# Softmax of a sparse attention: maxima subtracted by VectorE into SBUF, one exponential per kind of head and pair, row sums by VectorE

## The chip, the core and the metric

The kernel runs on one core of a Trainium2 chip. A core has TensorE (matmuls, PE in the profile), VectorE (DVE), ScalarE (ACT), GpSimd (POOL) and SyncE (SP), which issues the DMAs. Matmuls write into PSUM, here eight banks of 128 x 512 float32; SBUF is the working memory. The metric is the device time of one execution in microseconds; a kernel's time is the median of its runs.

## The reference

It is an attention with sparse masks, followed by two expert layers on its output. `q`, `k` and `v` have the shape 4 x 8 x 576 x 64; the layers have 2304 tokens of width 512 and 2048 hidden features.

```python
scores = scale * np.matmul(q, k.transpose(0, 1, 3, 2))
rel = pos[:, None] - pos[None, :]
mask_local = (rel >= 0) & (rel < 32)
mask_strided = (rel >= 0) & (pos[None, :] % 32 == pos[:, None] % 32)
# heads 0 to 3 take mask_local, heads 4 to 7 mask_strided
scores = np.where(masks[None], scores, -1e9)
scores = scores - np.max(scores, axis=-1, keepdims=True)
attn = np.exp(scores)
attn = attn / (np.sum(attn, axis=-1, keepdims=True) + 1e-09)
x = heads_side_by_side(np.matmul(attn, v))
h = x @ moe_w_in;  x = (h * sigmoid(1.702 * h)) @ moe_w_out
h = x @ moe2_w_in; return (h * sigmoid(h)) @ moe2_w_out
```

## The kernel before

The work is cut into eight chunks, one for each batch and half of the sequence. In each chunk `attention(c, b)` computes the attention and `chunk(c)` the first layer for its 288 tokens; the second layer follows for all tokens, from about 500 us on. Chunk 0 runs in float32. From chunk 1 on each operand is split into a high and a low float16 half, and a product takes three matmuls.

A chunk's attention has four pairs: pair `i` joins local head `i` (g = 0) and strided head `i` (g = 1). A local head has three blocks of 96 queries by 128 keys. A strided head has four blocks of 72 x 72 in a first half (s = 0) and five of 63 x 126 in a second half (s = 1); of these five, four lie in one PSUM bank and one in another. There are 32 pairs in all, 16 for each half.

A pair passes these steps. TensorE writes mask and scores into PSUM banks (`scores`, L643 and L662). VectorE takes the negated row maxima (`maxes`, L671). The maxima are multiplied by the score scale (`scaled`, L681 on ScalarE or L683 on VectorE). ScalarE then runs one exponential for each block, seven or eight a pair (`exps`, L690): it reads the bank, adds the scaled maximum as a bias, writes to `sml` (local) or `sms` (strided) in SBUF, and collects the row sum through its accumulator into `sus`. VectorE adds 1e-9 to the sums and divides by a power of two, PSC (L696), and takes the reciprocal (L699). GpSimd multiplies the probabilities by it (L708). TensorE transposes them (L715), ScalarE or VectorE brings them from the bank to `ptt` (L722 to L730), VectorE makes the low half (L732), and TensorE multiplies with v (`times_v`, L757 for chunk 0, L764 else). The results go to `x` (L784 to L797).

In `chunk`, sixteen hidden tiles of the first layer take twelve matmuls each (L846; L843 in chunk 0), with the activation on ScalarE (L854) and the split on ScalarE (L383) and VectorE (L390). The second product has sixteen groups of twelve (L877; L873 in chunk 0). Beside this run the conversions of the first layer's weights (ScalarE L429 and L281, VectorE L286 and L288, GpSimd L293, norms on TensorE L301), their splits (L390), the parking of the second layer's weights in HBM and the sums that its fast products need ("factors", L505 and L528).

The order of all this is made ahead by a `Planner`, a list scheduler: every step is a task with a cost in microseconds for each engine that may run it, a priority (a due time), the tasks that it follows, and the buffers that it takes and uses. Eight PSUM banks are one pool (`ps`), the score tiles are the pools `sl` and `st` of four slots each. Where two engines are given, the one that comes free first takes the task. So a change of costs or of dependences moves other tasks too. Each engine works through its list in order. In this first part the planner's order is final for all five engines; the second layer has a planner of its own.

## Time and profile before

| | |
|---|---|
| median of 3 runs | 891.87 us (891.73 to 893.89) |
| span of the profiled execution, first to last instruction | 885.8 us |
| TensorE busy | 852.4 us, 96% |
| VectorE busy | 669.3 us, 76% |
| ScalarE busy | 591.8 us, 67% |
| GpSimd busy | 415.7 us, 47% |
| TensorE busy from 30 to 66, 66 to 91 and 433 to 500 us | 36.00, 23.39 and 66.87 us |

The profiled execution's own time outside its span is not given; the median of the runs is 6.1 us above the span. Busy time counts stretches in which at least one instruction of the engine is under way. Matmuls overlap one another, so a busy TensorE is not yet one at its full rate, and the rate of its groups is read beside it. A wait names the engine and line whose semaphore came last. The chain follows the work that ended last back to its cause, step by step.

### The profile page before, as it was taken

The numbers are of one execution on the slowest core, as the hardware profiler recorded it, in microseconds if no ns is written. First come the engines' busy times: TensorE is split into PE (matmuls) and PEld (weight loads), VectorE is DVE, ScalarE is ACT, GpSimd is POOL, SyncE is SP. The second block draws the span as 40 slices with busy tenths as digits, with TensorE's granted clock in tenths as the row PEclk, the third lists the DMA queues.
The fourth block names the chain that finished last, engine by engine and source line by source line (L and its number), as shares of the span: only waits on it lengthen the run. The fifth ranks groups of instructions, "written<-read, shape, count | busy, mean of one in ns | idle before, by whom it ended". The sixth has DMA issues, their size and how long they took to land.

```text
span 885.8 us, 21399 instructions
## 1 busy us (share of the span) xinstructions
PE 852.4 (96%) x8198; PEld 720.9 (81%) x8198; DVE 669.3 (76%) x1198; ACT 591.8 (67%) x1410; POOL 415.7 (47%) x430
## 2 busy tenths in 40 slices
PE   5999897899999899999999999999999999999997
PEld 4976675787888787788888888888888998888886
DVE  3798888988659778999475372788888699968742
ACT  5788688999959979899469342464555487646420
POOL 4666664553322345965222162577887563212110
PEclk9999999999999999999999999999999999999999
DMA  9857443455337277384210283467676989756501
GB/s 316 255 176 207 132 127 100 127 174 187 97 103 211 84 242 236 119 250 163 71 50 9 77 322 108 165 225 232 200 231 205 309 274 304 255 179 211 195 36 48
DMA packets 86086, 155.27 MB, mean 175 GB/s; under 512 B 8416, under 2 KB 45792, under 8 KB 84960
## 3 DMA queue, kind: packets, MB, share of 16 engines
q1 hardware_dynamic: 85984, 153.91, 53.6%
q8 instruction: 64, 1.05, 0.5%
q14 instruction: 38, 0.31, 0.1%
HBM read 100.40 MB, written 53.48 MB: 174 GB/s over the span
## 4 chain that ended last, share of the span: by engine, by line
PE 72%; DVE 11%; ACT 8%; DMA 4%; issue 2%; POOL 1%; SPq 0%; DVEq 0%; ACTq 0%; POOLq 0%
PE aps L1157 9%; PE aps L1268 8%; PE aps L877 6%; PE aps L846 5%; PE gps L877 5%; PE hps L1157 5%; PE gps L1157 4%; PE hps L1268 4%; PE gps L1268 4%; PE hps L846 3%; PE gps L846 2%; DMA rk<-in_k_dram 2%; PE hps L877 2%; ACT sms L690 1%; ACT sml L690 1%
## 5 line engine op out<-in xcount | busy, mean ns | idle before, releaser
L1157 PEld LDWEIGHTS <-wf 128*128 128x128 f16 x1680 | 150.6, 98 | 15.3
L1268 PEld LDWEIGHTS <-wf 128*128 128x128 f16 x1512 | 147.6, 98 | 18.6 <-issue 1.1
L846 PEld LDWEIGHTS <-regA 128*128 128x128 f16 x1152 | 113.1, 99 | 37.0 <-issue 5.3
L877 PEld LDWEIGHTS <-regB 128*128 128x128 f16 x1152 | 108.7, 98 | 27.4 <-issue 0.5
L973 POOL TENSOR_TENSOR tt<-tt 128x256 f32<-128x256 f32 (+2 forms) x84 | 74.7, 900 | 47.2 <-DVE wf L980 17.7
L846 PE MATMUL aps<-x,regA 128*128 128x288 f16 x600 | 80.0, 287 | 1.8 <-DVE g L390 1.4
L877 PE MATMUL aps<-g,regB 128*128 128x288 f16 x576 | 77.7, 286 | 0.5 <-ACT sml L690 0.5
L968 ACT ACTIVATE wf<-tt,xsg 128x512 f16<-128x512 f32 x87 | 58.1, 713 | 26.5 <-PE hps L1268 7.0
L293 POOL TENSOR_TENSOR wm<-wm 128x512 int32<-128x512 int32 x32 | 42.8, 1336 | 64.0 <-DVE wm L288 45.8
L980 DVE SCALAR_TENSOR_TENSOR wf<-tt,xsg,wf 128x512 f16<-128x512 f32 x87 | 71.5, 870 | 0.0
L708 POOL TENSOR_TENSOR sml<-sml,sus 96x384 f32<-96x384 f32 x32 | 30.4, 950 | 82.2 <-DVE sus L699 69.5
L877 PE MATMUL gps<-g,regB 128*128 128x288 f16 x432 | 58.9, 286 | 0.0
L1268 PE MATMUL aps<-regA,wf 128*128 128x256 f16 x456 | 53.2, 273 | 0.1
L1157 PE MATMUL aps<-xfa,wf 128*128 128x256 f16 (+1 forms) x528 | 53.1, 256 | 0.0
L1169 ACT ACTIVATE tt<-tt 128x512 f32<-128x512 f32 x39 | 24.4, 625 | 29.4 <-DVE tt L1164 29.3
L846 PE MATMUL gps<-x,regA 128*128 128x288 f16 x288 | 40.4, 291 | 3.3 <-DVE g L390 1.7
L968 ACT ACTIVATE wf<-regB,xsg 128x512 f16<-128x512 f32 x39 | 27.0, 715 | 19.6 <-DMA regB<-g_scratch 8.3
L1157 PE MATMUL aps<-g,wf 128*128 128x256 f16 x324 | 38.8, 273 | 0.0
L846 PE MATMUL hps<-x,regA 128*128 128x288 f16 x264 | 35.6, 286 | 1.6 <-DVE wm L288 1.6
L1268 PE MATMUL aps<-regB,wf 128*128 128x256 f16 x312 | 37.0, 273 | 0.0
L708 POOL TENSOR_TENSOR sms<-sms,sus 72x288 f32<-72x288 f32 (+1 forms) x32 | 34.5, 1079 | 0.0
L1268 PE MATMUL hps<-regA,wf 128*128 128x256 f16 x264 | 32.4, 273 | 0.8 <-DVE x L1283 0.5
(365 smaller groups left out, 2155.3 us busy)
## 6 DMA issues: line engine op xcount, KB each, us to landing
tt<-g_scratch SPq DMA_DIRECT2D x76, 256.0 KB, 4.1
g_scratch<-tt SPq DMA_DIRECT2D x64, 256.0 KB, 2.8
w<-in_moe_w_out_dram SPq DMA_DIRECT2D x24, 512.0 KB, 4.4
rv<-in_v_dram SPq DMA_DIRECT2D x8, 1024.0 KB, 5.2
regB<-in_moe_w_in_dram SPq DMA_DIRECT2D x16, 512.0 KB, 8.4
w<-in_moe_w_in_dram SPq DMA_DIRECT2D x16, 512.0 KB, 3.7
w_scratch<-wm SPq DMA_DIRECT2D x32, 256.0 KB, 3.1
regB<-g_scratch SPq DMA_DIRECT2D x32, 256.0 KB, 4.1
```

Source lines behind the costliest of these rows:

```text
L293: nc.gpsimd.tensor_tensor(out=di, in0=m.bitcast(I32), in1=di, op=ALU.add)
L690: nc.scalar.activation(out=sm[0:nq, e * nk:e * nk + nk], in_=bank[0:nq, (e % 4) * nk:(e % 4) * nk + nk], func=AF.Exp, bias=nms[0:nq, sl.id ...
L708: nc.gpsimd.tensor_tensor(out=smv(), in0=smv(), in1=sus[0:nq, sl.idx, 3 * g:3 * g + nb, None].to_broadcast([nq, nb, nk]), op=ALU.mult), [k ...
L846: nc.tensor.matmul(o, lhsT=pvA[:, f, x, kk, :], rhs=x1[:, y, kk, :], start=(i == 0), stop=(i == 3 * KD - 1))
L877: nc.tensor.matmul(o, lhsT=pvB[:, f, u, dt * 128:(dt + 1) * 128], rhs=g1[:, w, f, :], start=(f == 0 and j == 0), stop=(f == KF - 1 and j = ...
L968: nc.scalar.activation(out=out, in_=in_, func=AF.Copy, scale=s)
L973: return P.add({e: x for e, x in any_add(n).items() if e in by}, prio, lambda on: (nc.gpsimd if on == "POOL" else nc.vector).tensor_tensor ...
L980: dve_t(n), prio, lambda on: nc.vector.scalar_tensor_tensor(out=lo(), in0=src(), scalar=s(), in1=hi(), op0=ALU.mult, op1=ALU.subtract),
L1157: nc.tensor.matmul(place(b, f), lhsT=wf[:, nf * g + f, x, wa, 128 * kk:128 * kk + 128], rhs=rhs.rearrange("p (h t) -> p h t", h=2) if n2 = ...
L1169: return P.add(act_t(512), t + 5, lambda on: nc.scalar.activation(out=sl(b), in_=sl(b), func=AF.Silu), after, (), [b], tab="silu")
L1268: nc.tensor.matmul(bank(b)[:, 256 * half:256 * half + 256], lhsT=fb[:, x, a, 128 * f:128 * f + 128], rhs=wt[:, 4 * p + f, z, wi, :], start ...
```

## The change

The maxima are no longer scaled. For each bank VectorE adds the negated maxima to the scores, with the maxima broadcast along the keys, and writes the result into `sml` or `sms` (`shifted`, L690 of the new kernel). ScalarE then runs one exponential for all blocks of a kind of head, from SBUF to SBUF in place, with the score scale and without bias or accumulator (`exps`, L698). VectorE sums the rows (`row_sums`, L702). The rows in `sml` and `sms` are one element longer; the last element is 1e-9, written once at the start by GpSimd, so that the sum has the constant in it. The reciprocal follows at once (L715), and the power of two is now multiplied in where the transposed probabilities leave their bank (L737 to L748). The tasks follow one another separately for the two kinds of head, and their costs are new.

```diff
-    sml = at.tile([LQ, NSM, NLB * 128], F32, name="sml")
-    sms = at.tile([72, NSM, 630], F32, name="sms")
+    sml = at.tile([LQ, NSM, NLB, 128 + 1], F32, name="sml")
+    sms = at.tile([72, NSM, 5, 126 + 1], F32, name="sms")
...
+    nc.gpsimd.memset(sml[:, :, :, 128], 1e-9)
+    nc.gpsimd.memset(sms[:, :, :, 126], 1e-9)
...
+        def probs(g, sl, st, s):
+            nq, nk, blocks = geom(s, g == 1)
+            x = sms[0:nq, st.idx, 0:len(blocks)] if g else sml[0:nq, sl.idx]
+            return x[:, :, x.shape[2] - 1 - nk:]
...
-            knm = P.add({"ACT": 0.22, "DVE": 0.22}, t + 2.2, scaled, kmx, (), [sl])
-            def exps(on, g, e):
...
-                nc.scalar.activation(
-                    out=sm[0:nq, e * nk:e * nk + nk], in_=bank[0:nq, (e % 4) * nk:(e % 4) * nk + nk], func=AF.Exp,
-                    bias=nms[0:nq, sl.idx, 3 * g + e:3 * g + e + 1], scale=sc_t[c]["s"][0:nq] if c else qscale,
-                    accum_out=sus[0:nq, sl.idx, 3 * g + e:3 * g + e + 1])
-            kx = [[P.add({"ACT": 0.39}, t + 3 + 2 * g, lambda on, g=g, e=e: exps(on, g, e), [knm], (),
-                         [sl, *([st, bs[e // 4]] if g else [bl])], tab="exp") for e in range(n_st if g else 3)] for g in range(2)]
-            krc = P.add({"DVE": 0.2}, t + 7, lambda on: nc.vector.tensor_scalar(
-                out=sus[:, sl.idx, 0:n8], in0=sus[:, sl.idx, 0:n8], scalar1=1e-9, scalar2=1.0 / PSC,
-                op0=ALU.add, op1=ALU.mult), kx[0] + kx[1], (), [sl])
+            def shifted(on, g):
+                nq, nk, blocks = geom(s, g == 1)
+                for e0, bank in zip((0, 4), [bl] if not g else bs):
+                    n = min(len(blocks) - e0, 4)
+                    nc.vector.tensor_tensor(
+                        out=probs(g, sl, st, s)[:, e0:e0 + n, 0:nk],
+                        in0=banks[bank.idx][0:nq, 0:n * nk].rearrange("p (b k) -> p b k", k=nk),
+                        in1=nms[0:nq, sl.idx, 3 * g + e0:3 * g + e0 + n, None].to_broadcast([nq, n, nk]), op=ALU.add)
+
+            def exps(on, g):
+                nq, nk, blocks = geom(s, g == 1)
+                x = probs(g, sl, st, s)[:, :, 0:nk]
+                nc.scalar.activation(out=x, in_=x, func=AF.Exp, scale=sc_t[c]["s"][0:nq] if c else qscale)
+
+            def row_sums(on, g):
+                nq, nk, blocks = geom(s, g == 1)
+                nc.vector.tensor_reduce(out=sus[0:nq, sl.idx, 3 * g:3 * g + len(blocks)], in_=probs(g, sl, st, s),
+                                        axis=AX.X, op=ALU.add)
+
+            ks = []
+            for g in range(2):
+                nq, nk, blocks = geom(s, g == 1)
+                n = len(blocks) * nk
+                kd = P.add({"DVE": 0.08 * (1 + s * g) + 0.00106 * n}, t + 2.2, lambda on, g=g: shifted(on, g), [kmx[g]], (),
+                           [sl, *([st, *bs] if g else [bl])])
+                ke = P.add({"ACT": 0.2 + 0.00083 * n}, t + 3 + 2 * g, lambda on, g=g: exps(on, g), [kd, *([k_scale_q[c]] if c else [])], (),
+                           [st if g else sl], tab="exp")
+                ks.append(P.add({"DVE": 0.08 + 0.00106 * n}, t + 5 + 2 * g, lambda on, g=g: row_sums(on, g), [ke], (),
+                                [sl, *([st] if g else [])]))
...
-                            nc.scalar.activation(out=o, in_=x, func=AF.Copy)
+                            nc.scalar.activation(out=o, in_=x, func=AF.Copy, scale=PSC)
...
-                    kp = P.add({"DVE": 0.42}, t + 13 + g, lambda on, p=p, pb=pb, n=n, nk=nk: nc.vector.tensor_tensor(
-                        out=ptt[0:nk, pb.idx, 1, 0:n], in0=banks[p.idx][0:nk, 0:n], in1=ptt[0:nk, pb.idx, 0, 0:n],
-                        op=ALU.subtract), [kp], (), [p, pb])
+                    kp = P.add({"DVE": 0.42}, t + 13 + g, lambda on, p=p, pb=pb, n=n, nk=nk: nc.vector.scalar_tensor_tensor(
+                        out=ptt[0:nk, pb.idx, 1, 0:n], in0=banks[p.idx][0:nk, 0:n], scalar=PSC, in1=ptt[0:nk, pb.idx, 0, 0:n],
+                        op0=ALU.mult, op1=ALU.subtract), [kp], (), [p, pb])
```

How this moves the work is shown at three places. In the rows below `hps`, `gps` and `aps` are PSUM banks, `nms` the maxima, `sus` the sums and reciprocals, `g` the hidden values, `wm` and `w` weights under conversion.

VectorE at the start of the program, before: the first pair's way from its maxima to its reciprocal.

```order
L671 TENSOR_REDUCE nms<-hps 96x3
L671 TENSOR_REDUCE nms<-hps 72x4
L671 TENSOR_REDUCE nms<-gps 96x3
L671 TENSOR_REDUCE nms<-gps 72x4
L683 TENSOR_SCALAR nms<-nms 96x7
L671 TENSOR_REDUCE nms<-aps 96x3
L671 TENSOR_REDUCE nms<-aps 72x4
L683 TENSOR_SCALAR nms<-nms 96x7
L696 TENSOR_SCALAR sus<-sus 96x7
L699 RECIPROCAL sus<-sus 96x7
```

The first reciprocal is the tenth of these rows. VectorE now: the last twelve of the 21 rows from the first maximum to the first reciprocal.

```order
L678 TENSOR_REDUCE nms<-aps 96x3
L678 TENSOR_REDUCE nms<-aps 72x4
L690 TENSOR_TENSOR sml<-aps,nms 96x3x128
L690 TENSOR_TENSOR sms<-aps,nms 72x4x72
L702 TENSOR_REDUCE sus<-sml 96x3
L678 TENSOR_REDUCE nms<-aps 96x3
L678 TENSOR_REDUCE nms<-aps 72x4
L690 TENSOR_TENSOR sml<-aps,nms 96x3x128
L690 TENSOR_TENSOR sms<-aps,nms 72x4x72
L702 TENSOR_REDUCE sus<-sms 72x4
L702 TENSOR_REDUCE sus<-sml 96x3
L715 RECIPROCAL sus<-sus 96x7
```

The maxima and subtractions of all four pairs and two sums of later pairs stand ahead of it. TensorE between chunk 0's last matmuls (L873, second product) and what follows, before:

```order
L873 MATMUL hps<-g_78,regB 128x288
L873 MATMUL gps<-g_78,regB 128x288
L873 MATMUL aps<-g_78,regB 128x288
L643 LDWEIGHTS idb
L643 MATMUL aps<-mL,idb 96x128
```

and now:

```order
L889 MATMUL hps<-g_78,regB 128x288
L889 MATMUL aps<-g_78,regB 128x288
L889 MATMUL gps<-g_78,regB 128x288
L780 LDWEIGHTS vz
L780 MATMUL gps<-ptt,vz 128x96
```

Before, mask and scores of three pairs of attention 2 (L643, L662) came here; now the products of attention 1 with v (L780), after which chunk 1's hidden matmuls begin, and attention 2's scores come later. VectorE at the first hidden tiles of chunk 1, before:

```order
L390 SCALAR_TENSOR_TENSOR g_78<-aps,sg,g_78 128x288
L390 SCALAR_TENSOR_TENSOR vz<-rv,s,vz 128x16x64
L390 SCALAR_TENSOR_TENSOR g_78<-gps,sg,g_78 128x288
L390 SCALAR_TENSOR_TENSOR regB<-regB,s 128x512
L671 TENSOR_REDUCE nms<-hps 96x3
L671 TENSOR_REDUCE nms<-hps 72x4
L390 SCALAR_TENSOR_TENSOR g_78<-aps,sg,g_78 128x288
```

and now:

```order
L392 SCALAR_TENSOR_TENSOR g_78<-aps,sg,g_78 128x288
L392 SCALAR_TENSOR_TENSOR regB<-regB,s 128x512
L392 SCALAR_TENSOR_TENSOR g_78<-aps,sg,g_78 128x288
L392 SCALAR_TENSOR_TENSOR g_78<-hps,sg,g_78 128x288
L392 SCALAR_TENSOR_TENSOR g_78<-gps,sg,g_78 128x288
L392 SCALAR_TENSOR_TENSOR regB<-regB,s 128x512
L286 TENSOR_SCALAR aps<-wm 128x512
```

The maxima of attention 2 no longer stand between the low halves of the first hidden tiles. In both programs the second layer's instructions are the same in kind and number.

## Rows read from the trace of the kernel before

**Rows 1.** The page's head and busy times: engine, us, share, instructions.

```profile
span 885.8 us, 21399 instructions
...
PE 852.4 (96%) x8198; PEld 720.9 (81%) x8198; DVE 669.3 (76%) x1198; ACT 591.8 (67%) x1410; POOL 415.7 (47%) x430
```

**Rows 2.** Busy us per stretch: length, PE, PEld, DVE, ACT, POOL, PEclk, DMA share, GB/s.

```profile
0.00:30.00 30.00, 20.64 (x147) 18.50 (x147) 12.58 (x32) 16.57 (x71) 13.41 (x33) 1.00 0.94 303
...
91.00:115.00 24.00, 21.26 (x192) 16.70 (x191) 20.39 (x40) 15.68 (x41) 13.83 (x14) 1.00 0.33 106
115.00:148.00 33.00, 27.07 (x283) 20.69 (x282) 28.47 (x52) 28.28 (x79) 19.63 (x17) 0.95 0.41 112
148.00:205.00 57.00, 53.20 (x538) 43.06 (x537) 50.96 (x103) 53.22 (x142) 25.85 (x24) 1.00 0.50 152
205.00:262.00 57.00, 57.00 (x599) 46.35 (x598) 38.12 (x86) 46.53 (x128) 20.03 (x17) 1.00 0.38 125
262.00:319.00 57.00, 54.02 (x589) 44.73 (x587) 46.17 (x98) 50.93 (x136) 20.20 (x20) 1.00 0.53 159
319.00:376.00 57.00, 55.57 (x588) 45.28 (x587) 51.44 (x101) 49.77 (x139) 37.32 (x36) 1.00 0.62 193
376.00:433.00 57.00, 57.00 (x601) 46.82 (x599) 50.33 (x93) 49.02 (x140) 31.63 (x32) 1.00 0.56 178
```

**Rows 3.** From the chain, in order of time: start us, us, what (two hidden tiles).

```profile
392.65 2.94 PE hps L846 x24
```

**Rows 4.** TensorE's waits up to 500 us: us in total, times, longest.

```profile
PE aps L715 <- DVE wm L288: 2.7, 1, 2.7
...
PE gps L846 <- DVE g L390: 1.7, 1, 1.7
...
PE hps L643 <- ACT sml L690: 0.6, 1, 0.6
```

**Rows 5.** VectorE by line: count, busy us, mean ns; or ns min/median/max.

```profile
L671 DVE TENSOR_REDUCE nms<-aps 96x3 f32<-96x384 f32 x17 | 9.2, 544 | 2.1 <-PE aps L662 2.1
...
L671 DVE TENSOR_REDUCE nms<-hps 63x4 f32<-63x504 f32 x7 | 4.6, 659 | 0.0
...
L671 DVE TENSOR_REDUCE nms<-aps 63x1 f32<-63x126 f32 x11 | 3.0, 270 | 0.0
...
L496 DVE TENSOR_REDUCE w2a<-acc 128x1 f32<-128x16 f32 x2 | 0.3, 156 | 0.0
...
L696 DVE TENSOR_SCALAR sus<-sus 96x7 f32<-96x7 f32 (+1 forms) x32 | 11.0, 343 | 10.7 <-ACT sms L690 10.6
...
L696 DVE TENSOR_SCALAR sus<-sus x32: 151/168/2466, 16.1 to 487.3; 96x7 f32<-96x7 f32 x16, 96x8 f32<-96x8 f32 x16
...
L732 DVE TENSOR_TENSOR ptt<-aps,ptt x23: 396/454/489, 96.1 to 493.4; 128x288 f16<-128x288 f32 x10, 126x315 f16<-126x315 f32 x8, 72x288 f16<-72x288 f32 x5
```

**Rows 6.** ScalarE: five exponentials with their reads (chain); L968 by form.

```profile
475.76 2.18 ACT sms L690 x10
...
L968 ACT ACTIVATE wf<-tt,xsg 128x512 f16<-128x512 f32 x87 | 58.1, 713 | 26.5 <-PE hps L1268 7.0 <-DMA tt<-g_scratch 6.7 <-POOL tt L973 5.1
...
L968 ACT ACTIVATE regA<-regB,s 128x256 f16<-128x256 f32 x14 | 7.0, 502 | 7.9 <-DMA regB<-w_scratch 7.6 <-POOL regB L973 0.3
```

**Rows 7.** The start, in order of time (the last row from the chain).

```profile
12.44 0.92 DVE L671 TENSOR_REDUCE nms<-gps 96x3 f32<-96x384 f32 x2 [1.28 <-PE gps L662]
...
16.68 0.82 POOL L708 TENSOR_TENSOR sml<-sml,sus 96x384 f32<-96x384 f32 x1 [10.09 <-DVE sus L699]
...
19.96 0.66 POOL L708 TENSOR_TENSOR sms<-sms,sus 72x288 f32<-72x288 f32 x1
...
21.37 0.47 PE hps L757 x2
```

**Rows 8.** TensorE at chunk 1's first hidden tiles, in order of time.

```profile
137.63 2.75 PE L846 MATMUL gps<-x,regA 128*128 128x288 f16 x12 [1.56 <-DVE x L797]
140.18 3.69 PE L846 MATMUL aps<-x,regA 128*128 128x288 f16 x24
```

22 lines of the change are left out of this document (7 added, 15 removed).

## The prediction

> **What bounds the kernel now.** I read the page's totals first. TensorE is busy 96% of the span of 885.8 us [rows 1], VectorE and ScalarE far less; a share of the whole says little where stages differ, so the next view is the busy time by stretch. The second expert layer (from about 500 us on) holds no instruction that the change touches: between the two programs every count there is the same. Up to 500 us TensorE idles for 28 us in all: 9.36 in the first 30 us, 2.74 and 5.93 from 91 to 148 us, then 3.80, 0, 2.98, 1.43 and 0 in stretches of 57 us [rows 2], and 1.7 in the three stretches that aren't shown. So TensorE is the bound, and a gain can only come out of those 28 us; the start, where it waits for the first load, gives little of it back. A busy TensorE is also working at its rate: twelve matmuls of 288 columns follow each other every 1.47 us, 122 ns each, and 288 columns at 2.4 GHz take 120 [rows 3].
>
> The view of the waits says on whom TensorE waits. The longest behind the start are on VectorE, 2.7 us on the bits of a converted weight (L288) and 1.7 on the low half of a hidden value (L390); the longest on an exponential (ScalarE L690) is 0.6 [rows 4]. That speaks against a plain reading of the change: it relieves ScalarE, on which TensorE waits seldom, and loads VectorE, on which it waits more.
>
> **What it does to the engines' work.** The counts are those of the two orders, 32 pairs (head pair and half), 16 of each geometry; the durations are rows.
>
> VectorE, added: one subtraction for each maximum, same bank, same shape. No such operation is in the trace. The nearest rows are the maxima, 0.544 us for 96x384, 0.659 for 63x504, 0.270 for 63x126, so 0.96 ns an element between the first two and 0.45 us for 72x288, and the subtraction at L732, which also reads a bank and an SBUF tile, 0.396 to 0.489 for 288 to 315 columns [rows 5]. By the maxima: 32 x 0.544 + 16 x 0.45 + 16 x (0.659 + 0.270) = 39.5 us. The row sums read SBUF. The only reduction from SBUF in the trace takes 0.156 us for 16 elements [rows 5]; with the maxima's slope 387, 292 and 635 elements take 0.51, 0.42 and 0.75 us, 35 us in all. Priced as maxima from a bank it would be 37. I take 36. Together +75 us.
>
> VectorE, removed: L696, which added the constant, 32 instructions, 11.0 us [rows 5], and the 18 scalings of maxima that ran there (L683), the same operation on as small a tile, 18 x 0.34 = 6. The planner also moves choices: 16 evictions of transposed probabilities to ScalarE (-7.2 at 0.45), seven squares net (-7.8), three additions to GpSimd (-2.0). The last three are counts of the orders by the nearest durations (squares 0.5 to 1.7 us). Net 75 - 17 - 17 = **+41 us on VectorE**.
>
> ScalarE, removed: 240 exponentials. Five of them with their five accumulator reads take 2.18 us [rows 6], so 240 x 0.436 = 105 us. Added: 64 from SBUF to SBUF. The nearest row is L968, 0.713 us for 512 elements and 0.502 for 256 with a scale from a column [rows 6], so 0.61, 0.53 and 0.81 us for 384, 288 and 630 elements, 40 us. The 14 scalings that ran here (4), four table loads fewer (5), 16 more evictions (+7), squares and splits that come over (+10, all by the nearest durations) leave **-57 us on ScalarE**. GpSimd keeps its 64 normalisations; what it gains and loses is below 3 us. The exact power of two moves from the reciprocal into the evictions, where it is one more operand of the same instruction: nothing. The two memsets run between 4.8 us and GpSimd's first normalisation at 16.68 us [rows 7], where it is idle.
>
> One thing is in doubt here. L696 has a median of 0.168 us and a maximum of 2.466, while L732 stays between 0.396 and 0.489 [rows 5]: some VectorE instructions are held up and others not. If the row sums are held up as L696 was, by 0.343 - 0.168 = 0.175 us on the mean, VectorE gets 64 x 0.175 = 11 us more. I take nothing for it, since L732 is nearer in kind to the subtractions, and keep 11 for the range. The Trainium skill, page "SBUF — State Buffer", section on who interferes with whom, says that an instruction in a two-port mode locks with GpSimd while a reduction on this chip never does; by that the sums keep 36 us and L696's hold-ups go with it, by the other reading they would be 47. The trace agrees on L696; it has no large reduction from SBUF.
>
> **What of it reaches TensorE.** I go stretch by stretch.
>
> Start, 0 to 36 us. Chunk 0's softmax was ScalarE's work for the most part; now it is VectorE's, and the order puts other pairs' work ahead of the first pair's end. The second pair's maxima start at 12.44 us, when its scores are there [rows 7]; the first pair's maxima and subtractions fit ahead of that. Then come its maxima 0.92 and subtractions 0.98, a sum 0.51, then maxima, subtractions and a sum of the third pair 2.41, maxima and subtractions of the fourth 1.90, sums 0.42 and 0.51, reciprocal 0.19. That is 20.3 us, and GpSimd can begin the first pair there instead of at 16.68. It takes 0.82 + 0.66 us a pair, so the second pair leaves it at about 23.3 instead of 20.6 (19.96 + 0.66), and the products with v, which started at 21.37 us [rows 7], start nearly 3 us later. Norm matmuls that the new order puts into the gap give 0.7 back later. Chunk 0's matmuls follow without a gap from 36 us, so it is carried on: **+2.5 us** (bounds 0 and 4).
>
> 66 to 148 us. VectorE is busy 20.4 of 24 and 28.5 of 33 us here [rows 2], it converts weights and does attention 1. The four pairs of attention 1 now cost it some 9 us more. But three of the four score groups of attention 2, which stood ahead of chunk 1's first matmuls, now come after thirteen of its sixteen hidden tiles: 3.3 us of matmuls and some 4 us of VectorE leave this stretch; and about 6 us of chunk 0's softmax now lie ahead of 23 us, where VectorE sat idle. The idle 2.74 and 5.93 us are thus likely to shrink; I take half, **-4.3** (bounds 0 and -8.7). With it goes part of a clock loss: the mean granted clock from 115 to 148 us is 0.95, so part of it ran at 1.2 GHz, and after the lull twelve matmuls took 2.75 us and the next 24 took 3.69 [rows 2, 8], where at the rate of [rows 3] they take 1.6 and 3.1, the last one's tail included. Half of 1.7 us is **-0.8**.
>
> 148 to 205 us: VectorE 50.96 of 57 [rows 2], less of attention 2 in it early and more late: 0 (-3.8 to +3). 205 to 262: TensorE is full and VectorE has 38 us; the planner fills that room, and by counts and durations it comes to about 59 us there: **+2** (0 to 4). 262 to 376: idle 2.98 and 1.43, with chains through squares, splits and exponentials on ScalarE, which now has a quarter less to do, and part of VectorE's work gone to the chunk before: **-3** (0 to -4.4). After that TensorE is full before and has nothing to give: 0 (to +4, where VectorE's 50.33 of 57 gets its 5 us on top).
>
> Sum: +2.5 - 4.3 - 0.8 + 0 + 2 - 3 = -3.6 us. The profiled execution's span is 885.8 us; the median of the three runs is 891.87, so 6.1 us lie around the span, and I leave them as they are. 885.8 - 3.6 + 6.1 = **888.3 us**.
>
> **Rivals.** First, **VectorE becomes the bound**. Per chunk it gets 41 / 8 = 5 us more; in the stretches from 148, 319 and 376 us it was busy 50.96, 51.44 and 50.33 of 57 [rows 2]. If it needs the idle 6 us that it had there (it waits in order for ScalarE, now also for each exponential, and everything behind a row sum waits with it), each of the three grows by 5 us, less the 3.80 and 1.43 us that TensorE idled already: +10, with the start's 2.5 and nothing won before 148 us about +12, 904 us; if it can live with half of that idle time, +4, 896. It decides from the point where VectorE's idle time in these stretches can't fall below 3 us. For it: nearly all of TensorE's long waits are on VectorE. Against it: the stretches from 205 and 262 us have 19 and 11 us of room [rows 2], and parking and factors can move there.
>
> Second, **the tuned part was hidden**: TensorE full, what is won at 91 to 148 us is lost at the start, 891 within 2 us. For it: 0 idle in two of the stretches shown [rows 2]. Third, **the idle time mostly goes**: -8.7, -1.7, -3.8 and -4.4 with +2.5 at the start, 16 us at most; two thirds of it give 881. For it: hold-ups of up to 2.47 us at L696 [rows 5] go, and banks are free once subtracted, no longer after seven or eight exponentials.
>
> **How the numbers follow.** The forecast's case, some of the idle time regained, 39% (885 to 889); hidden 25%; mostly gone 11%; VectorE bound 25%. About 0.3%, 2.7 us, is what a measurement of this kernel can tell from no change. The forecast's case reaches a little into that: faster 0.47, same 0.27, slower 0.26. The range leaves a tenth at either side: from 879 (the third case's better half left out) to 899 (between the first rival's two prices).
>
> **What would show it.** Right: ScalarE's busy time some 50 us lower and VectorE's 35 to 45 higher with all of it ahead of 500 us; the first product with v near 24 us; chunk 1's first hidden matmul (137.63 us before [rows 8]) earlier by 2 to 4 us; TensorE's idle time up to 500 us near 25 us. Wrong: row sums over 0.6 us for 387 elements, a start that gives back its delay, or VectorE busy over 55 of 57 us with TensorE waiting on L390 and on transposes, which is the first rival.

## Result, and the profile after the change

| | before | after |
|---|---|---|
| median of the runs | 891.8 us (887.39 to 893.89, 4 runs) | 878.65 us (873.83 to 879.21, 4 runs) |
| ratio | | 0.9845, interval 0.9812 to 0.9878 |
| span of the profiled execution | 885.8 us | 876.6 us |
| VectorE, ScalarE busy | 669.3, 591.8 us | 694.1, 537.5 us |

The change makes the kernel 13 us faster. A second measurement of the same two kernels, beside some of the experiments, gives 0.9837 (0.9807 to 0.9866). The forecast was 888.3 us with a range from 879.0 to 899: the direction was right, the time lies just below the range, and the gain is more than three times the 3.6 us of the sum.

The page of the changed kernel, its head and busy times (as [rows 1]):

```profile
span 876.6 us, 21029 instructions
...
PE 850.7 (97%) x8198; PEld 721.6 (82%) x8198; DVE 694.1 (79%) x1259; ACT 537.5 (61%) x1009; POOL 417.3 (48%) x432
```

The busy time by stretch, columns as in [rows 2]:

```profile
0.00:30.00 30.00, 18.54 (x131) 16.40 (x132) 17.88 (x42) 16.14 (x31) 16.13 (x37) 1.00 0.94 308
...
66.00:91.00 25.00, 22.98 (x174) 17.45 (x172) 24.63 (x42) 22.49 (x38) 17.21 (x13) 1.00 0.77 225
91.00:115.00 24.00, 22.85 (x215) 17.79 (x214) 22.67 (x40) 12.47 (x22) 12.47 (x11) 1.00 0.26 79
115.00:148.00 33.00, 32.20 (x253) 24.82 (x254) 31.46 (x59) 25.74 (x53) 22.17 (x20) 1.00 0.34 98
148.00:205.00 57.00, 52.90 (x565) 43.32 (x564) 53.25 (x101) 40.78 (x90) 30.10 (x27) 0.97 0.51 162
205.00:262.00 57.00, 57.00 (x640) 46.92 (x639) 52.34 (x112) 45.97 (x92) 24.52 (x19) 1.00 0.52 160
262.00:319.00 57.00, 57.00 (x598) 47.19 (x596) 46.45 (x108) 42.36 (x89) 24.93 (x23) 1.00 0.49 164
319.00:376.00 57.00, 57.00 (x640) 46.93 (x638) 51.56 (x103) 44.22 (x87) 30.97 (x34) 1.00 0.56 171
376.00:433.00 57.00, 57.00 (x595) 46.95 (x594) 46.69 (x94) 42.74 (x90) 30.14 (x31) 1.00 0.53 175
```

TensorE's idle time in a stretch is its length less the first number: 2.74 and 5.93 us from 91 to 148 us [rows 2] have become 1.15 and 0.80, and 2.98 and 1.43 us from 262 to 376 us have become 0. The start idles 11.46 us instead of 9.36. VectorE is busier in all of these stretches but that from 376 us on, and TensorE still waits less.

What TensorE waits for up to 500 us (as [rows 4]):

```profile
PE hps L650 <- POOL mL L342: 3.9, 1, 3.9
PE hps L730 <- POOL sml L723: 3.8, 1, 3.8
PE hps L669 <- DMA rk<-in_k_dram: 3.7, 2, 2.7
PE hps L650 <- DVE wm L288: 1.6, 1, 1.6
...
PE aps L893 <- DVE sml L690: 1.2, 1, 1.2
...
PE hps L650 <- DVE g L392: 0.8, 1, 0.8
```

The first three lie in the first 21 us. The wait on GpSimd's first normalisation (L730) is 3.8 us where it was 1.2; that is what the longer way of the first pair costs. The wait on an exponential in [rows 4] is gone, that on a hidden value's low half (L390, now L392) is 0.8 instead of 1.7, and the new kind, on a bank that VectorE still subtracts from (L690), is short.

**Three marks.** Because a stretch of fixed length holds other work in each trace, I compare traces by three marks on TensorE: A, the start of chunk 0's second hidden tile; B, the first hidden matmul of chunk 1; C, the first matmul of the second layer. In the kernel before (A and C; B is in [rows 8]):

```profile
39.64 2.16 PE L843 MATMUL aps<-x,regA 128*128 128x288 f32 x8
...
501.80 2.37 PE L1001 MATMUL hps<-x,regA 128*128 128x288 f16 x18
```

In the changed kernel (the first row is chunk 0's first hidden tile, then B and C):

```profile
39.42 3.90 PE L859 MATMUL aps<-x,regA 128*128 128x288 f32 x8
...
132.31 1.84 PE L862 MATMUL aps<-x,regA 128*128 128x288 f16 x12
...
491.70 2.49 PE L1017 MATMUL hps<-x,regA 128*128 128x288 f16 x19
```

A is 43.15 us there. In its second trace, from another execution of the same kernel:

```profile
37.01 2.16 PE L859 MATMUL aps<-x,regA 128*128 128x288 f32 x8
...
127.84 1.84 PE L862 MATMUL aps<-x,regA 128*128 128x288 f16 x12
...
487.13 2.12 PE L1017 MATMUL hps<-x,regA 128*128 128x288 f16 x16
```

| | A | A to B | B to C | C to the end | span |
|---|---|---|---|---|---|
| before | 39.6 | 98.0 | 364.2 | 384.0 | 885.8 |
| after | 43.2 | 89.2 | 359.4 | 384.9 | 876.6 |
| after, second trace | 39.0 | 88.8 | 359.3 | 384.9 | 872.0 |

Between the two traces of the changed kernel only A differs, by 4.1 us; the rest agrees within 0.4. So the gain has two places, A to B (chunk 0's matmuls and attention 1) and B to C (chunks 1 to 7). But 8.8 us less from A to B are not 8.8 us won there, since work has moved behind B with the scores of attention 2. The busy time between the marks, columns as in [rows 2], before:

```profile
39.64:137.63 97.99, 89.43 (x732) 69.34 (x730) 86.10 (x150) 78.98 (x187) 65.01 (x52) 1.00 0.54 168
137.63:501.80 364.17, 354.11 (x3703) 288.70 (x3703) 281.32 (x571) 302.38 (x825) 155.85 (x147) 1.00 0.43 135
```

and now:

```profile
43.15:132.31 89.16, 85.24 (x637) 65.68 (x636) 78.04 (x140) 63.57 (x114) 55.64 (x42) 1.00 0.48 145
132.31:491.70 359.39, 355.24 (x3793) 291.67 (x3789) 303.96 (x627) 262.31 (x534) 163.85 (x153) 1.00 0.44 139
```

From A to B TensorE has 637 matmuls instead of 732 and is busy 4.2 us less; its idle time there falls by 4.6 us, from 8.56 to 3.92. From B to C it has 90 matmuls more, and its idle time falls by 5.9 us, from 10.06 to 4.15. So both places give about as much. The 0.9 us behind C are not the change's: C to the end is 384.0 or 384.9 us in traces of either program (384.9 with run 3 below, which has the steps of before, 384.1 with run 17, which has the new ones).

### The profile page after: what moved, and what is told of

Its sections match the earlier page's. It is cut to its first block, busy times and chain, and to the rows that moved or that the text cites. A ratio compares the mean times of both kernels' runs of the same rounds, so it can differ in the third digit from the quotient of the medians.

```text
span 876.6 us, 21029 instructions
## 1 busy us (share of the span) xinstructions
PE 850.7 (97%) x8198; PEld 721.6 (82%) x8198; DVE 694.1 (79%) x1259; ACT 537.5 (61%) x1009; POOL 417.3 (48%) x432
## 4 chain that ended last, share of the span: by engine, by line
PE 83%; DVE 9%; DMA 2%; issue 2%; POOL 1%; ACT 1%; SPq 0%; DVEq 0%; POOLq 0%
PE aps L1173 9%; PE aps L893 8%; PE aps L1284 8%; PE aps L862 7%; PE gps L893 5%; PE hps L1173 5%; PE gps L1173 4%; PE hps L1284 4%; PE gps L1284 4%; PE hps L893 3%; PE gps L862 3%; PE hps L862 3%; PE aps L859 2%; DMA tt<-g_scratch 2%; PE aps L669 2%
## 5 line engine op out<-in xcount | busy, mean ns | idle before, releaser
L1284 PEld LDWEIGHTS <-wf 128*128 128x128 f16 x1512 | 147.6, 98 | 19.5 <-issue 2.0
L862 PE MATMUL aps<-x,regA 128*128 128x288 f16 x636 | 84.3, 286 | 0.0
L293 POOL TENSOR_TENSOR wm<-wm 128x512 int32<-128x512 int32 x32 | 45.8, 1430 | 60.9 <-DVE wm L288 47.1
L893 PE MATMUL gps<-g,regB 128*128 128x288 f16 x336 | 45.7, 286 | 0.0
L1173 PE MATMUL aps<-g,wf 128*128 128x256 f16 x324 | 38.8, 273 | 0.0
L862 PE MATMUL hps<-x,regA 128*128 128x288 f16 x264 | 35.6, 286 | 0.0
L862 PE MATMUL gps<-x,regA 128*128 128x288 f16 x252 | 34.2, 286 | 0.0
```

The lines of the kernel that those rows point to most:

```text
L293: nc.gpsimd.tensor_tensor(out=di, in0=m.bitcast(I32), in1=di, op=ALU.add)
L862: nc.tensor.matmul(o, lhsT=pvA[:, f, x, kk, :], rhs=x1[:, y, kk, :], start=(i == 0), stop=(i == 3 * KD - 1))
L893: nc.tensor.matmul(o, lhsT=pvB[:, f, u, dt * 128:(dt + 1) * 128], rhs=g1[:, w, f, :], start=(f == 0 and j == 0), stop=(f == KF - 1 and j = ...
L1173: nc.tensor.matmul(place(b, f), lhsT=wf[:, nf * g + f, x, wa, 128 * kk:128 * kk + 128], rhs=rhs.rearrange("p (h t) -> p h t", h=2) if n2 = ...
L1284: nc.tensor.matmul(bank(b)[:, 256 * half:256 * half + 256], lhsT=fb[:, x, a, 128 * f:128 * f + 128], rhs=wt[:, 4 * p + f, z, wi, :], start ...
```

## Experiments

Each trace is of one execution, and A moves by itself (last section), so A to B and B to C are compared across kernels, and the ratio has the last word. A trace can also have a stretch of a few microseconds at a granted clock of 0.50, which is 1.2 GHz, between two marks where another has none. All traces in one table:

| kernel | ratio to before, interval | A | A to B | B to C |
|---|---|---|---|---|
| before | 1 | 39.6 | 98.0 | 364.2 |
| changed | 0.9845, 0.9812 to 0.9878 | 43.2 | 89.2 | 359.4 |
| 1 before, costs corrected | 1.0070, 1.0042 to 1.0098 | 41.5 | 90.6 | 378.5 |
| 2 before, scores of attention 2 later | 1.0002, 0.9980 to 1.0025 | 39.9 | 102.1 | 365.1 |
| 3 before without L696 | 0.9989, 0.9959 to 1.0019 | 38.8 | 98.2 | 366.1 |
| 4 changed, banks held | 0.9883, 0.9834 to 0.9933 | 39.4 | 88.9 | 364.8 |
| 5 changed, copies in the chain | 1.0018, 0.9998 to 1.0039 | 40.9 | 90.7 | 370.5 |
| 6 changed, copies aside | 0.9900, 0.9869 to 0.9931 | 43.1 | 92.1 | 362.1 |
| 7 changed, row sums twice | 1.0118, 1.0083 to 1.0152 | 45.0 | 95.5 | 375.6 |
| 8 changed, one exponential a block | 0.9961, 0.9943 to 0.9978 | 41.2 | 96.6 | 361.0 |
| 9 old in chunks 0 to 2 | 0.9948, 0.9925 to 0.9970 | 41.4 | 97.1 | 360.0 |
| 10 old in chunks 3 to 7 | 0.9850, 0.9793 to 0.9907 | 38.6 | 90.8 | 362.3 |
| 11 new in chunk 1 alone | 0.9921, 0.9895 to 0.9946 | 39.3 | 90.4 | 368.5 |
| 12 old in chunk 1 alone | 0.9892, 0.9861 to 0.9923 | 42.7 | 97.8 | 355.2 |
| 13 old in chunk 0 alone | 0.9881, 0.9840 to 0.9922 | 40.5 | 92.1 | 360.4 |
| 14 changed, first pair first | 0.9872, 0.9838 to 0.9906 | 42.1 | 91.6 | 363.5 |
| 15 changed, banks held in chunks 0 and 1 | 0.9903, 0.9872 to 0.9934 | 38.5 | 88.8 | 367.0 |
| 16 changed, squares on ScalarE | 0.9827, 0.9793 to 0.9860 | 42.5 | 89.2 | 361.9 |
| 17 changed, scores of attention 2 sooner | 0.9831, 0.9803 to 0.9859 | 43.9 | 89.2 | 363.7 |

My theories at the start were two: "work" (ScalarE's 54 us less bring the gain) against "order" (the new place of attention 2's scores and of what goes with it).

### Is it the order alone? (1 and 2)

```diff
-            kx = [[P.add({"ACT": 0.39}, ...
+            kx = [[P.add({"ACT": 0.436}, ...
-            krc = P.add({"DVE": 0.2}, t + 7, lambda on: nc.vector.tensor_scalar(
+            krc = P.add({"DVE": 0.35}, t + 7, lambda on: nc.vector.tensor_scalar(
```

> The kernel before with two numbers of its plan corrected to what the trace of before shows: an exponential of a block costs 0.436 us instead of 0.39, the constant 0.35 instead of 0.2. No instruction is added or removed; only the order changes, and by it three of the four score groups of attention 2 come behind thirteen hidden tiles of chunk 1, as in the changed kernel. If the gain came from the order (theory 'order'), TensorE's idle time from 91 to 148 us falls from 8.7 us to 2 to 4, and the time to some 0.992 to 0.995 of before. If it came from the work taken off ScalarE (theory 'work'), it stays within 1.5 us of 8.7 and the time within 0.3% of before.

```diff
             ready = [k_q, k_load[c, "s"], ...
+            if c == 2:
+                ready.append(h_done[1][12])
```

> The kernel before, its costs untouched, with one dependence more: the scores of attention 2 wait for the thirteenth hidden tile of chunk 1. Theory 'order': chunk 1's first hidden matmul moves from 137.6 us to some 133, idle time from 91 to 148 us falls by 4 to 7 us, the time to 0.993 to 0.996 of before. Theory 'work': VectorE and ScalarE still reach attention 1's end as late as before, the first hidden matmul stays within 1.5 us of 137.6 less the 3.3 us of score matmuls that lie behind it now, idle time up by as much, and the time within 0.3%.

Moving the scores alone gives nothing: 1.0002, B later instead of sooner. Two rows by stretch of that kernel show why:

```profile
91.00:115.00 24.00, 21.27 (x148) 16.19 (x148) 16.63 (x34) 11.40 (x30) 12.60 (x12) 0.79 0.28 88
115.00:148.00 33.00, 27.39 (x224) 20.23 (x222) 27.60 (x52) 28.48 (x76) 20.53 (x18) 0.90 0.51 148
```

TensorE idles 2.73 and 5.61 us there, as before, since VectorE and ScalarE bring attention 1 to its end no sooner, and the granted clock falls to a mean of 0.79 and 0.90, so part of the stretch ran at 1.2 GHz. Corrected costs do more: A to B is 90.6 us, nearly that of the changed kernel, with the old instructions. But B to C takes 378.5 us, and the kernel is 0.7% slower than before:

```profile
148.00:205.00 57.00, 50.52 (x547) 41.37 (x546) 48.47 (x102) 47.18 (x141) 28.88 (x24) 0.88 0.45 145
205.00:262.00 57.00, 54.65 (x559) 44.41 (x558) 41.35 (x90) 50.24 (x128) 19.48 (x18) 1.00 0.41 133
```

Neither of these is what the theory "order" said of the time. Still, half of it stands: most of what the changed kernel wins between A and B can be had by order, without less work (TensorE idles 4.83 us there, 8.56 before, 3.92 in the changed kernel). True costs as such don't make a better order.

### Which engine's work counts? (5, 6, 7)

```diff
                 nc.scalar.activation(out=x, in_=x, func=AF.Exp, scale=...)
+                nc.scalar.activation(out=x, in_=x, func=AF.Copy)
```

> The changed kernel in its own order, with ScalarE given some 40 us back: behind each exponential it copies the probabilities onto themselves (64 instructions of some 0.6 us, unknown to the plan). VectorE's row sums wait that much longer. Theory 'work': the idle time from 91 to 148 us and from 262 to 376 us, 1.95 and 0 us in the changed kernel, goes back to some 5 and 3 to 4.4, the time to 0.992 to 0.997 of before (5 to 10 us over the changed kernel). Theory 'order': both stay below 1.5 us over the changed kernel's, and the time within 2 us of it (0.984 to 0.988 of before).

```diff
                 nc.scalar.activation(out=x, in_=x, func=AF.Exp, scale=...)
+                n = len(blocks)
+                nc.scalar.activation(out=jk[0:nq, 0:n * nk].rearrange("p (b k) -> p b k", k=nk),
+                                     in_=idt[0:nq, None, 0:nk].to_broadcast([nq, n, nk]), func=AF.Copy)
```

> The changed kernel in its own order; ScalarE copies a constant of the exponential's shape to a scratch tile behind each exponential, 64 instructions and some 40 us, but no row sum, no normalisation and no bank waits for the copies themselves. Theory 'throughput' (ScalarE's work as such costs): as much is lost as with the copies in the chain, 10 to 15 us, 0.996 to 1.003 of before. Theory 'latency' (the copies hurt because each row sum comes 0.6 us later): at most 4 us over the changed kernel, 0.984 to 0.989.

```diff
+                for _ in range(2):
                     nc.vector.tensor_reduce(out=sus[...], in_=probs(g, sl, st, s), axis=AX.X, op=ALU.add)
```

> The changed kernel in its own order, every row sum made twice (64 more VectorE instructions, some 35 us; unknown to the plan). If VectorE has room (theory 'ScalarE', by which only ScalarE's 40 us counted), the time stays within 3 us of the changed kernel, 0.984 to 0.988 of before. If VectorE, busy 46 to 53 of 57 us from 148 us on, has none, TensorE's idle time grows there by 8 us or more and the time goes to 0.994 or above.

The added instructions, in the view of groups by line. The copies in the chain:

```profile
L699 ACT ACTIVATE sms<-sms 72x288 f32<-72x288 f32 (+1 forms) x32 | 18.8, 588 | 1.0
...
L699 ACT ACTIVATE sml<-sml 96x384 f32<-96x384 f32 x32 | 16.8, 524 | 1.0
```

The copies aside:

```profile
L700 ACT ACTIVATE jk<-idt 96x384 bf16<-96x384 f32 x64 | 34.5, 539 | 0.0
```

The row sums made twice, where half of the 128 are added, some 37 us:

```profile
L703 DVE TENSOR_REDUCE sus<-sms 72x4 f32<-72x292 f32 (+1 forms) x64 | 39.8, 624 | 1.1
...
L703 DVE TENSOR_REDUCE sus<-sml 96x3 f32<-96x387 f32 x64 | 35.1, 548 | 3.8 <-ACT sml L698 2.7
```

35.6 us of copies in the chain cost the whole gain (1.0018). 34.5 us of the same work aside cost a third of it (0.9900). So ScalarE's time as such, which the theory "work" named, is the smaller part of this loss: most of it comes from the row sums that come later. Both losses are larger than I had forecast (0.992 to 0.997 for the copies in the chain, at most 0.989 for those aside). Of the 11.1 us that the copies in the chain add between B and C (370.5 against 359.4), the copies aside add 2.7. Between A and B both cost little, 1.5 and 2.9, and each of the two traces has 3.4 us at a granted clock of 0.50 there, the changed kernel's none. 37 us more of VectorE's work cost 1.0118 - 0.9845 = 2.7%, 24 us; 22.5 of them stand between the marks (A to B 6.3, B to C 16.2). These sums stand in the chain as well, and no run put such work beside it, so whether VectorE lacks room or the chain is late is not separated here. Behind 205 us TensorE then waits on what comes last in a pair's chain, the low half of the transposed probabilities. The longest wait there with the copies in the chain:

```profile
PE aps L781 <- DVE ptt L749: 2.2, 1, 2.2
```

and with the sums twice:

```profile
PE aps L781 <- DVE ptt L749: 3.2, 2, 3.0
```

That chain can be measured: from a pair's last score matmul to the end of its reciprocal, over the 28 pairs of chunks 1 to 7, paired in order of time. The mean is 13.3 us before (median 10.6), 8.2 and 8.1 in the two traces after (median 7.4 and 7.3), 8.9 with copies aside, 9.9 with copies in the chain, 10.6 with the sums twice. Before, that chain holds maxima, their scaling, seven or eight exponentials, L696 and the reciprocal; now maxima, subtractions, two exponentials, the sums and the reciprocal. The chain's length alone doesn't set the time, though: with the old steps in chunks 3 to 7 (run 10) its mean is 10.7 us, longer than in any of these three, and the gain is kept (0.9850). The order of run 10 was made with the old steps in it; the copies and second sums of runs 5 to 7 are unknown to the order. So what these runs show is what work costs that the order doesn't know, in the chain and beside it.

### Which part of the change? (3, 4, 8)

```diff
-            krc = P.add({"DVE": 0.2}, t + 7, lambda on: nc.vector.tensor_scalar(
-                out=sus[...], in0=sus[...], scalar1=1e-9, scalar2=1.0 / PSC, op0=ALU.add, op1=ALU.mult), kx[0] + kx[1], (), [sl])
+            krc = P.add({"DVE": 0.2}, t + 7, lambda on: None, kx[0] + kx[1], (), [sl])
...
-                            nc.vector.tensor_copy(out=o, in_=x)
+                            nc.vector.tensor_scalar(out=o, in0=x, scalar1=PSC, scalar2=None, op0=ALU.mult)
```

> The kernel before in its own order without the 32 instructions of L696 (the constant 1e-9 is left out, the power of two moves into the evictions, as in the changed kernel): VectorE has 11.0 us less to do and one instruction less between the accumulators and the reciprocal. Theory 'VectorE is short' (35 us more of its work cost over 20 us in the run with the row sums twice): 3 to 7 us less, 0.992 to 0.997 of before. If VectorE's time counts only in the changed kernel's order, the time stays within 0.3% of before.

```diff
-                           [st if g else sl], tab="exp")
+                           [*([st, *bs] if g else [sl, bl])], tab="exp")
```

> The changed kernel with one line of its plan changed: a score bank is held until the exponential has run, as before, not only until VectorE has subtracted the maxima. Same instructions. If the earlier release of banks carries the gain: 0.992 to 1.000 of before, with TensorE idle again ahead of mask matmuls (L650). If it doesn't: 0.982 to 0.989.

```diff
-                nc.scalar.activation(out=x, in_=x, func=AF.Exp, scale=...)
+                for e in range(len(blocks)):
+                    nc.scalar.activation(out=x[:, e], in_=x[:, e], func=AF.Exp, scale=...)
-                ke = P.add({"ACT": 0.2 + 0.00083 * n}, ...
+                ke = P.add({"ACT": 0.2 * len(blocks) + 0.00083 * n}, ...
```

> The changed kernel with one exponential a block again (240 instead of 64, SBUF to SBUF, without bias and accumulator), with their cost in the plan: one part of the change undone. ScalarE gets some 40 us back (240 x 0.35 - 40). Theory 'ScalarE': most of the gain is lost, 0.993 to 1.002 of before. Rival (the plan, knowing the cost, works round it, and the gain came from banks that come free earlier): 0.984 to 0.990.

L696 with its hold-ups [rows 5] was worth nothing that can be measured; A to B and B to C are within 2 us of those of the kernel before. Banks that come free earlier carry little that shows: held as before, the kernel keeps 0.9883 (0.9834 to 0.9933, so that half of the gain goes with them isn't excluded), with the same A to B and 5.4 us more between B and C in its trace. One exponential a kind is the part that matters: with one a block again, three quarters of the gain go. They go between A and B, and two rows show how. In that kernel's list mask and scores of a pair of attention 2 stand ahead of chunk 1's hidden tiles, and their operand, the low half of k (L392), comes late from VectorE:

```profile
136.91 0.26 PE L669 MATMUL hps<-kh,qh 64*96 64x128 f16 x1 [3.31 <-DVE kh L392]
...
137.85 2.58 PE L863 MATMUL hps<-x,regA 128*128 128x288 f16 x10
```

B is 137.85 us, that of the kernel before. So in this trace the longer exponentials act on A to B by way of the order that the planner then makes; what they would cost in the changed kernel's own order isn't shown.

### Which chunks? (9 to 13)

The edit is one condition: `if c < 3:`, `c >= 3`, `c != 1`, `c == 1` or `c == 0` chooses the old steps (scaled maxima, one exponential a block from the bank with accumulator, the addition of 1e-9) with their old costs; the power of two stays in the evictions.

```diff
+            if c < 3:
+                knm = P.add({"ACT": 0.22, "DVE": 0.22}, t + 2.2, scaled, kmx, (), [sl])
+                kx = [P.add({"ACT": 0.39}, t + 3 + 2 * g, ... block_exps ..., tab="exp") ...]
+                ks = [P.add({"DVE": 0.2}, t + 7, ... tensor_scalar(... scalar1=1e-9 ...), kx, (), [sl])]
+            else:
                 for g in range(2):
```

> The changed kernel with the old softmax in chunks 0 to 2 (12 of 32 pairs), the mirror of the run with chunks 3 to 7 old. Gain pair by pair: some 60% stays, 0.988 to 0.993 of before, 262 to 433 us without idle time. Gain from the first 150 us: 0.997 to 1.002.

> The changed kernel with the old softmax in chunks 3 to 7 (20 of 32 pairs). If the gain comes pair by pair out of a shorter way from scores to reciprocal, some 40% of it stays: 0.990 to 0.995 of before, and TensorE idles 3 us or more from 262 to 433 us, where the changed kernel idles 0. If it comes from the first 150 us (weights under conversion, VectorE full): 0.984 to 0.988.

> The new softmax in chunk 1 alone (4 of 32 pairs), the old one in chunks 0 and 2 to 7. Theory 'attention 1' (the gain before chunk 1's hidden tiles comes from attention 1, whose exponentials and conversions of weights stand on the same two engines): chunk 1's first hidden matmul at 129 to 134 us instead of 137.6, and 5 us or more of the gain stay, 0.985 to 0.994 of before. Theory 'chunk 0 or 2': the first hidden matmul stays near 137 us, the time above 0.996.

> The mirror: the changed kernel with the old softmax in chunk 1 alone. Theory 'attention 1': first hidden matmul back at 136 to 140 us (132.3 in the changed kernel), the gain behind it kept, 0.991 to 0.996 of before. Theory 'chunk 0 or 2': below 134 us, the time within 2 us of the changed kernel.

> The changed kernel with chunk 0's softmax the old way (scaled maxima, seven exponentials a pair from the banks, accumulators); chunks 1 to 7 as changed. The start gets back what the change cost it: idle time of the first 30 us 9.4 instead of 11.5 us, the first product with v at 21.4 instead of 23.3. If nothing else moves, the time is 2 us below the changed kernel (0.982 of before). Rival: the 6 us of VectorE's work that the change drew into the idle time ahead of 23 us were part of the gain from 66 to 148 us; then that stretch idles 1 to 3 us longer and the time is that of the changed kernel or up to 1 us above.

Among these kernels A to B is 90.4 to 92.1 us wherever chunk 1 is new and 97.1 to 97.8 wherever it is old; TensorE idles 3.9 to 5.8 us there and 8.0 to 8.5. So the first place is attention 1, as the theory "attention 1" said. Chunk 1 alone, an eighth of the pairs, brings half of the gain (0.9921); without it about two thirds are left (0.9892), more than I expected, because its trace has the shortest way from B to C of all, 355.2 us. Half and two thirds are more than the whole, so a chunk's share depends on the order around it. With chunks 0 to 2 old a third of the gain is left (0.9948), between the ranges of both theories. The five later chunks don't show in the time: with them old the ratio is 0.9850, though the trace has 2.9 us more between B and C and a chain of 10.7 us. I had expected 0.990 to 0.995 if each pair brought its share; 0.9850 speaks against that, though its interval ends at 0.9907.

Chunk 0 new against old went nearly as the rival said. Old, the first product with v starts at 22.03 us instead of 23.28, A to B is 2.9 us longer with TensorE idle for 5.8 us in it instead of 3.9, and the kernel is not faster (0.9881).

### Does a better start help, and is there a faster version? (14 to 17)

```diff
+            kmx = [P.add(..., [ksc, *first_rc[0:c == 0 and i > 1]], ...
```

> The changed kernel with one dependence more in chunk 0: the maxima of the third and fourth pair wait for the first pair's reciprocal. GpSimd begins the first pair near 15.5 instead of 19.87 us, the first product with v starts 2 to 4 us sooner than 23.28, chunk 0's first hidden matmul 1 to 3 us sooner than 39.42. If that is carried on, 0.981 to 0.983 of before. Rival: as in the run with chunk 0 the old way, the stretch from 91 to 148 us idles longer instead, and the time is that of the changed kernel or 2 us above.

```diff
+                           [*([st, *bs] if g else [sl, bl])] if c < 2 else [st if g else sl], tab="exp")
```

> The changed kernel with banks held until the exponential in chunks 0 and 1 only. With banks held everywhere the first hidden matmul came at 128.4 us, but the rest of the first layer took 364.7 us, 5.3 more than in the changed kernel. If the two halves add up: first hidden matmul at 128.4, the rest 359 to 361, 871 to 875 us, 0.977 to 0.983 of before. If the later half hangs on what the earlier leaves: 878 to 881 us, 0.985 to 0.989.

```diff
-        return P.add(act_t(n) | dve_t(n), prio, fn, after, (), uses)
+        return P.add(act_t(n), prio, fn, after, (), uses)
```

> The changed kernel with all sums of squares on ScalarE (before, the planner split them; VectorE made some 23 us of them). If VectorE's length is what now sets the later half of the first layer (35 us more of its work cost some 24 us), 20 us less of it gives 2 to 6 us: 0.977 to 0.982 of before. Rival: TensorE is full from 205 to 500 us already (idle 0), so nothing is left to win there, and ScalarE's 20 us more cost what 40 us aside cost, 2 to 4 us: 0.986 to 0.990.

```diff
-            t = b + tab["s"] + tab["step"] * i
+            t = b + (10.0 if c == 2 else tab["s"]) + tab["step"] * i
```

> The changed kernel with the due time of attention 2's scores 12 us sooner, so that they stand between chunk 1's hidden tiles 6 and 13 and no longer behind the thirteenth. The changed kernel idles 4.1 us from 148 to 205 us, on banks that VectorE still converts weights in or subtracts from (L650, L893). If attention 2 sooner takes these waits away: idle there 0 to 2 us, 0.979 to 0.983 of before. Rival: attention 2's maxima and subtractions come between the low halves of chunk 1's hidden tiles, TensorE waits on those instead, and the time is 0.984 to 0.992.

The first pair first brings its product with v only 0.86 us sooner (22.42), and nothing in the time. The better halves of two orders don't add up: with banks held in chunks 0 and 1, A to B is 88.8 but B to C 367.0, and 0.9903 is worse than either range that I had named. Fewer squares on VectorE (busy 675.4 us instead of 694.1) and earlier scores of attention 2 give 0.9827 and 0.9831, which can't be told from the changed kernel. No version here beats it clearly. The changed kernel itself, measured beside the kernels of 11, 12 and 15:

> The changed kernel itself, beside the three others of this call and the kernel before, for a second trace of it: first hidden matmul at 132.3 us, second layer from 491.7 us if both are fixed by the order, 0.981 to 0.988 of before.

It came out at 0.9837, with B at 127.84 us and C at 487.13: not fixed by the order, since A had moved by 4.1 us.

## Why the prediction was wrong, and where it was right

The sum took too little of what went. Three of its terms fell short, and what lies around the span was taken as fixed. The terms in us, with what the two first traces show (TensorE's idle time in each stretch):

| term | forecast | came |
|---|---|---|
| the start | +2.5 | +2.1 |
| 66 to 148 us | -4.3 | -6.3 |
| 148 to 205 us | 0 | +0.3 |
| 205 to 262 us | +2 | 0 |
| 262 to 376 us | -3 | -4.4 |
| the clock | -0.8 | 0 |
| what lies around the span, 6.1 us | 0 | -4.0 |

The step that failed is that of 66 to 148 us, by size and by its reason. I booked attention 1's new softmax as 9 us more for VectorE, laid the gain to the score groups that move and to chunk 0, and took half. Up to 500 us 19.5 us of idle time are left, where I had written 25. The runs show another cause: the new softmax in chunk 1 alone brings half of the whole gain (run 11), and moving the scores alone brings nothing (run 2).

**The work.** The prices held. The row sums, the subtraction and the exponential of a local head, by line in the changed kernel:

```profile
L702 DVE TENSOR_REDUCE sus<-sml 96x3 f32<-96x387 f32 x32 | 17.4, 544 | 2.4 <-ACT sml L698 2.3
...
L690 DVE TENSOR_TENSOR sml<-aps,nms 96x384 f32<-96x384 f32 x18 | 9.7, 541 | 0.0
...
L698 ACT ACTIVATE sml<-sml,sc 96x384 f32<-96x384 f32 x28 | 17.1, 612 | 4.6 <-DVE sml L690 4.2
```

I had 510, 544 and 610 ns. All subtractions come to 39.2 us (39.5 forecast), all row sums to 37.1 (36; 37 by the price of a maximum from a bank). ScalarE is busy 54 us less (57 forecast). VectorE is busy 24.8 us more, not 35 to 45. The durations of its instructions sum to 32.6 us more, where I had 41; the rest of the difference is that neighbours overlap: a maximum of 0.54 and one of 0.45 us show as 0.92 together, and a subtraction of 0.54 us that starts at 11.15 us is followed by the next at 11.62. So a sum of durations overstates the busy time, by some 0.07 us an instruction at these places.

**Hold-ups of the row sums.** Over the whole kernel the local row sums take

```profile
L702 DVE TENSOR_REDUCE sus<-sml x32: 535/544/553, 14.2 to 473.1; 96x3 f32<-96x387 f32 x32
```

and none is held up, where L696 reached 2466 ns [rows 5]; 31 of all 64 row sums ran beside an instruction of GpSimd. What the Trainium skill says on the page "SBUF — State Buffer", section on who interferes with whom, that a reduction on this chip never locks with GpSimd, agrees with this trace. The 11 us that I kept for the range were not needed.

**The start, +2.5: about right.** GpSimd began the first pair at 19.87 us (20.3 forecast), the first product with v at 23.28 (near 24). The terms as I wrote them give 2.0 to 2.3 and not 2.5 (2.7 to nearly 3, less 0.7). A delay at A is carried on whole, as the two traces of the changed kernel show, but A also moves by itself by more than these 2 us, 4.1 between those two. Starts that were 0.9 to 1.3 us sooner (runs 13 and 14) had 2.4 to 2.9 us more between A and B, with TensorE idle for 5.8 and 4.8 us there instead of 3.9; run 14's trace also has a granted clock of 0.50 from 116.9 to 120.3 us, where the changed kernel's has 1.00. So in these orders a better start was lost again before B.

**66 to 148 us, -4.3 and -0.8: the step that failed.** I took half of the idle time for lack of a reason to take more; 6.3 of 10.3 us went, 1.61, 2.74 and 5.93 having become 2.02, 1.15 and 0.80. B came at 132.31 instead of 137.63, with A 3.5 later. A reason for more was in the order that I had printed: before, three score groups of attention 2 filled a gap ahead of B which exists because attention 1 comes late. Afterwards attention 1's steps stand earlier on all engines (its second pair's reciprocal 51.5 us behind A instead of 57.5, its fourth 81.0 instead of 89.7), and less is left of the gap, though the score groups no longer fill it. I saw three groups move and priced them at 3.3 us of matmuls; between A and B TensorE is busy 4.2 us less. That work only moved behind B. What was won there came from attention 1, which ends sooner.

**148 to 205 us, 0: right.** TensorE idles 4.10 us there (3.80 before).

**205 to 262 us, +2: wrong.** VectorE is busy 52.34 us there, not 59, and TensorE idles 0. The +41 that came as +25 is part of this error.

**262 to 376 us, -3: right in place and sign.** 4.41 us came, the whole idle time. But the reason that I gave, ScalarE's lighter load, explains little of it if work taken away counts as work added does (the copies aside cost 2.7 us from B to C), and the new softmax in those chunks isn't needed for the time (run 10). What else makes this stretch shorter in the changed kernel, other than that it follows another beginning, these runs don't settle.

**What lies around the span, 6.1 us: wrong.** Each run that lists both has 1.7 to 2.4 us there (878.42 against a span of 876.6). By an estimate from these the profiled execution of before took about 887.6 us, at the lower end of its executions (886.97 to 896.62), and I set its span against the median of others. So some 4 of the 6.1 us were what a typical execution took longer than the profiled one, and the change took them away: the changed kernel's median lies 2.0 us above its span. I had left them as they were. For a typical execution the gain is larger than the 9.2 us between the two spans first shown: 13.2 and 14.8 us between medians, 13.8 between the trace of before and the second one after.

**The clock, -0.8.** In the profiled executions the dip didn't shrink; it moved from 115 to 148 us (0.95) to 148 to 205 us (0.97). Over executions it is more: the mean granted clock of the 67 executions of before that ran beside these experiments, 0.987 to 0.998, has a mean of 0.993; the eight of the changed kernel lie at 0.997 and 0.998. Of the 67, those at 0.994 or above take 890.2 us on the mean, those at 0.991 or below 893.5. So the likely cause of those 4 us is that idle time that is gone also spares lulls behind which TensorE runs at 1.2 GHz; the trace of before, at 0.998, didn't show them.

**The rivals.** VectorE as the bound (904 or 896) fell for the kernel as it is: 53.25, 51.56 and 46.69 us of 57 in the three stretches that I named, and no stall on it behind 205 us. Its condition, less than 3 us of idle time left, was nearly met in the first of them (3.75 us). With VectorE busy 19 us less the time is the same (run 16), so VectorE doesn't bind the kernel as it is; 37 us more in the chain make it slower than before (run 7). The third rival, idle time that mostly goes (881), was the closest to what happened; I gave it 11%.

**What stays open.** Whether attention 1's earlier end comes from less work or from another order can't be fully separated: undoing the change in chunk 1 moves B back (12), but the old instructions with other costs reach B as early (1), and the changed order bears 35 us more of ScalarE's work with 1.5 us lost there (5). I take the order that the new steps lead to as the nearer cause, but that is argued and not shown; chunk 1 old with corrected costs, which would tell, was not tried. And the 5.9 us less of idle time from B to C have no cause that these runs show.

## What to carry to other kernels

Where a planner orders the work, read what the change does to the end of the stage that the bound engine waits for, before halving the idle time there by habit; here three fifths of it went. Work that the order doesn't know costs more in the chain from input to result than beside it: 35 us in the chain cost what 35 us beside it cost three times over. With the chain's steps in the plan, a longer chain cost nothing that shows (run 10). Compare a profiled span with its own execution's time, and take two traces before a few microseconds at one place are believed.
